# The head of a fused SSM and MLP kernel: x slabs loaded in token halves, a weight block in one load, a bias row first in its queue, a shorter warm-up

## The chip, the cores and the metric

The kernel runs on one core of one Trainium2 chip. The metric is device time in microseconds for one execution, end to end. The profile's own span is about 1.3 us shorter than that time (212.9 against 214.2 for the traced execution of before); spans are compared with spans and times with times. The experiments came in three batches, each on another chip and each with the kernel before measured again, so between batches the ratios are to be compared and not the times.

Names used below: PE is TensorE's matmul stream, PEld its weight loads, DVE is VectorE, ACT is ScalarE, SP and ACT also issue the transfers of the head ("SPq", "ACTq"). A "slab" is 128 of the 640 columns of x; a "W1 block" is the 128 rows of W1 that meet one slab.

## The reference, cut to what matters

For x of 2048 tokens by 640 features, the kernel gives g * a + (1 - g) * b, where b is an MLP and a is a diagonal state-space model:

```python
g = sigmoid((x * gate_w).sum(-1, keepdims=True))
b = gelu(x @ w1 + b1) @ w2 + b2            # w1: 640 x 1728, w2: 1728 x 640
# a: Bu = x @ B_bar.T, h[t] = Lam_bar * h[t-1] + Bu[t], y = 2 Re(h @ C.T) + x * Dskip
```

Everything is bf16 in and out.

## The kernel before: the parts that matter

Work on each engine is put in order at build time by a small scheduler; `op(name, engine, duration, reads, writes, fn, prio)` declares a piece of it, and `load(...)` a transfer. The head of the kernel:

```python
load("xna", "sp", ..., xn[0][:, :, 0:256], x2[0:512, 0:256] ...)       # slabs 0 and 1 of x, 512 tokens
for h in range(2):                                                       # W1 block 0, in two halves of its columns
    load(f"w1_0{h}", "sp", ..., W1sb[:, 0, fs], B_w1[0:128, fs], [("w1", 0, h)], ...)
w1load(1, "sp", 1.3)
w1load(2, "sp", 2)
xtrans(0, range(KN, KD), 3, 1.8)                                         # slabs 2 to 4, transposed by the DMA
w1load(3, "sp", 4)
w1load(4, "sp", 5)
...
def f_warm():                                                            # dummy matmuls, 3328 columns
    for n in (512,) * 6 + (256,):
        t = nc.tensor.matmul(PS[4][:, 0:n], one.broadcast_to([128, 128]), one.broadcast_to([128, n]), ...)
op("warm", "pe", 2.7, (), [("bank", 4)], f_warm, prio=-1000)
# slabs 0 and 1 are transposed on PE: 8 transposes, then copied from PSUM by DVE (3 copies)
for i, (k, c0, c1) in enumerate(((0, 0, 2), (0, 2, 4), (1, 0, 4))):
    ...
# the biases and the SSM's vectors sit in rows of one tile, and one PE transpose makes columns of them:
op("cols", "pe", 0.3, list(ROWS) + ["b1b", "ident"], [("bank", 7)], f_cols, prio=9.5)   # after 9 W1 matmuls
# then 40 matmuls of 512 columns, W1 block by W1 block (k), into 8 PSUM banks (jf):
#   (0,0..6), (1,0..6), (0,7), (1,7), (2,0..7), (3,0..7), (4,0..7)
```

The row tile is filled by five small loads on the ACT queue: three of 5 rows, one of 13 rows (the bias of the first 1664 hidden units), and last a single row for the remaining 64 hidden units, "b1b".

## Time and profile before

| | before |
|---|---|
| time, median of 4 executions | 213.85 us (213.47 to 213.9) |
| profiled span | 212.9 us |
| PE busy | 208.4 us, 98% |
| first W1 matmul | 4.64 us |
| start of the 12th W1 matmul | 8.30 us |

First, the page of the kernel before: busy time of each engine, share of the span, instructions.

```profile
PE 208.4 (98%) x1254; PEld 119.8 (56%) x1264; DVE 188.9 (89%) x262; ACT 111.3 (52%) x201; POOL 2.5 (1%) x10
```

PE is the bound. The chain of waits of the kernel before, in order of time (start, length, what), says where it isn't yet:

```profile
2.60 5.08 DMA rows<-in_B_b_dram
7.68 0.14 issue
7.82 0.22 PE ps L432
8.03 5.18 PE ps L621 x24
13.21 0.05 issue
13.27 1.46 PE ps L621 x6
```

From 2.60 to 7.68 us the chain is one transfer, the bias row b1b, which PE's bias transpose (line 432) waits for. From there to the end it is PE work with gaps of about 0.05 us. So a microsecond saved before about 9 us is worth a microsecond at the end, and nearly nothing else can be gained. The timeline of PE in the head of the kernel before (start, length, then in brackets the idle time before it and what ended it):

```profile
2.01 1.70 PE L401 MATMUL ps<-const-bfloat16-1.0 128*128 128x512 bf16 x4
3.74 0.65 PE L413 MATMUL ps<-ident,xn 128*128 128x128 bf16 x8
4.64 1.04 PE L621 MATMUL ps<-xT,W1sb 128*128 128x512 bf16 x4 [0.25 <-DVE xT L419]
5.85 0.82 PE L621 MATMUL ps<-xT,W1sb 128*128 128x512 bf16 x3 [0.17 <-DMA W1sb<-in_B_w_dram]
6.92 0.61 PE L621 MATMUL ps<-xT,W1sb 128*128 128x512 bf16 x2 [0.25 <-DMA W1sb<-in_B_w_dram]
7.82 0.22 PE L432 MATMUL ps<-ident,rows 128*128 128x128 bf16 x1 [0.29 <-DMA rows<-in_B_b_dram]
7.87 2.32 PE L621 MATMUL ps<-xT,W1sb 128*128 128x512 bf16 x10
```

Line 401 is the warm-up, 413 the transposes of x, 621 the W1 matmuls. Three holes follow the first W1 matmul: for the second half of block 0, for block 1, and for b1b. The brackets are smaller than the holes, because a matmul's recorded end lies some 0.16 us after the next one could have started (379 ns recorded, starts 0.2155 us apart). Counted by starts, the 12th W1 matmul begins 3.66 us after the first (8.30 - 4.64), where eleven matmuls of 0.2155 us and a bias transpose of 0.055 us need 2.43. So 1.24 us are lost in the holes. The view of one line, for the W1 matmuls between 4.5 and 9 us (durations in ns: least, median, largest), gives the speed:

```profile
L621 PE MATMUL ps<-xT,W1sb x15: 377/379/391, 4.6 to 8.9; 128*128 128x512 bf16 x15
```

All 15 take about 379 ns and start 0.2155 us apart when nothing is missing. The transfers, from the DMA view of the kernel before (size, then us from issue to landing; issued at 0.74, 1.25 and 1.79 us):

```profile
xn<-in_A_x_dram SPq DMA_DIRECT2D x1, 256.0 KB, 3.0
W1sb<-in_B_w_dram SPq DMA_DIRECT2D x1, 128.0 KB, 2.8
W1sb<-in_B_w_dram SPq DMA_DIRECT2D x1, 128.0 KB, 4.0
```

### The profile page before, as it was taken

Reading aid. Unit: us, or ns where it says so; the run is one execution under the profiler, and the core shown is the slowest. Engines: PE = TensorE matmul, PEld = TensorE weight load, DVE = VectorE, ACT = ScalarE, POOL = GpSimd, SP = SyncE. Lnnn points to the kernel's source line nnn. Section 1 sums busy time; section 2 is a strip of 40 time slices with the busy share of each in tenths; the row PEclk is TensorE's granted clock in tenths of the full one; section 3 lists DMA queues with packets and bytes.
Section 4 is the critical chain, followed back from the end, with each engine's and each line's share of the span. In section 5 each row is a group of like instructions: output and inputs, shape, how many; then the busy total and the mean of one; then the engine's idle time right before and its main releaser. Section 6 shows DMA issues by size and latency. Waiting matters only on the chain.

```text
span 212.9 us, 3113 instructions
## 1 busy us (share of the span) xinstructions
PE 208.4 (98%) x1254; PEld 119.8 (56%) x1264; DVE 188.9 (89%) x262; ACT 111.3 (52%) x201; POOL 2.5 (1%) x10
## 2 busy tenths in 40 slices
PE   8899999999999999999999999999999999999996
PEld 3344444444467776444466777544446777767773
DVE  2399999999999999999999959999999998999343
ACT  2389556678915324556963233555793444723330
POOL 1000000000000010000000001000000000000000
DMA  5999999998100004100000004000000000000011
GB/s 134 298 284 200 170 208 318 265 222 183 22 0 3 31 31 126 62 0 0 0 3 0 0 34 155 31 31 3 0 0 2 3 31 31 31 3 31 31 34 62
DMA packets 31434, 16.35 MB, mean 77 GB/s; under 512 B 22972, under 2 KB 30652, under 8 KB 31420
## 3 DMA queue, kind: packets, MB, share of 16 engines
q1 hardware_dynamic: 31072, 14.83, 29.2%
q0 software_dynamic: 288, 1.31, 1.9%
q8 instruction: 10, 0.16, 0.3%
q14 instruction: 4, 0.03, 0.0%
q10 hardware_dynamic: 60, 0.01, 0.0%
HBM read 7.63 MB, written 2.62 MB: 48 GB/s over the span
## 4 chain that ended last, share of the span: by engine, by line
PE 95%; DMA 2%; issue 1%; ACTq 1%; POOL 0%; DVE 0%; POOLq 0%
PE ps L771 27%; PE ps L641 22%; PE ps L819 20%; PE ps L684 20%; PE ps L621 3%; DMA rows<-in_B_b_dram 2%; PE ps L785 1%; PE ps L662 1%; ACTq L326 1%; DVE osb L852 0%; POOL io_i L382 0%; PE ps L432 0%; POOL rows L372 0%; POOL st_i L384 0%; POOL st_i L383 0%
## 5 line engine op out<-in xcount | busy, mean ns | idle before, releaser
L771 PE MATMUL ps<-W2sb,Gl 128*128 128x320 bf16 x416 | 59.2, 299 | 0.0
L771 PEld LDWEIGHTS ps<-W2sb,Gl 128*128 128x128 bf16 x416 | 40.3, 98 | 17.1 <-issue 1.1
L641 PE MATMUL ps<-xT,W1sb 128*128 128x512 bf16 x215 | 47.5, 379 | 0.3
L819 PE MATMUL ps<-CT,H 128*128 128x320 bf16 (+2 forms) x320 | 45.4, 299 | 0.0
L724 DVE TENSOR_TENSOR_SCAN W<-atab,V 128x1280 bf16<-128x1280 f32 x16 | 44.3, 2811 | 0.3
L684 PE MATMUL ps<-xT,BT 128*128 128x512 bf16 x196 | 43.1, 379 | 0.3 <-issue 0.2
L819 PEld LDWEIGHTS ps<-CT,H 128*128 128x128 bf16 x320 | 31.3, 98 | 12.2
L799 ACT ACTIVATE E<-ps,g1col 128x320 bf16<-128x320 f32 x32 | 16.3, 526 | 39.7 <-PE ps L771 26.0
L641 PEld LDWEIGHTS ps<-xT,W1sb 128*128 128x128 bf16 x220 | 21.5, 98 | 26.0
L648 ACT ACTIVATE Gl<-ps,cols 128x512 bf16<-128x512 f32 x44 | 29.6, 688 | 10.0 <-PE ps L641 10.0
L684 PEld LDWEIGHTS ps<-xT,BT 128*128 128x128 bf16 x200 | 19.5, 98 | 23.5 <-ACT Gt L670 0.4
L693 ACT ACTIVATE U<-ps 128x512 bf16<-128x512 f32 x40 | 23.8, 597 | 15.0 <-PE ps L684 14.9
L830 ACT ACTIVATE E<-ps,gcol 128x320 bf16<-128x320 f32 x30 | 15.8, 527 | 22.6 <-PE ps L819 22.6
L482 DVE TENSOR_TENSOR osb<-xg,E 128x640 bf16<-128x640 bf16 x15 | 7.3, 487 | 9.2 <-ACT E L830 8.2
L758 ACT ACTIVATE ps<-b2b 128x320 f32<-128x320 bf16 x32 | 14.1, 442 | 1.1
L838 DVE SCALAR_TENSOR_TENSOR xg<-xn,gcol,dsk 128x640 bf16<-128x640 bf16 x16 | 13.9, 883 | 0.4
L598 DVE SCALAR_TENSOR_TENSOR scr<-xn,gwb 128x640 bf16<-128x640 bf16 x16 | 13.2, 823 | 0.4
L482 DVE TENSOR_TENSOR V<-V,W 128x1280 bf16<-128x1280 bf16 x16 | 12.5, 822 | 0.3
L482 DVE TENSOR_TENSOR H<-H,V 128x1280 bf16<-128x1280 bf16 x16 | 12.5, 822 | 0.3
L482 DVE TENSOR_TENSOR V<-mr,U 128x2560 bf16<-128x2560 bf16 x8 | 11.9, 1489 | 0.2
L482 DVE TENSOR_TENSOR H<-c,W 128x2560 bf16<-128x2560 bf16 x8 | 11.9, 1489 | 0.1
L482 DVE TENSOR_TENSOR V<-s,W 128x2560 bf16<-128x2560 bf16 x8 | 11.9, 1485 | 0.0
(79 smaller groups left out, 98.5 us busy)
## 6 DMA issues: line engine op xcount, KB each, us to landing
out_dram<-osb SPq DMA_DIRECT2D x15, 160.0 KB, 1.8
W2sb<-in_B_w_dram SPq DMA_DIRECT2D x1, 2080.0 KB, 9.4
xn<-in_A_x_dram POOLq DMA_DIRECT2D x2, 640.0 KB, 4.7
W1sb<-in_B_w_dram SPq DMA_DIRECT2D x4, 256.0 KB, 4.8
xn<-in_A_x_dram SPq DMA_DIRECT2D x1, 640.0 KB, 8.0
W1sb<-in_B_w_dram SPq DMA_DIRECT2D x1, 480.0 KB, 5.7
W1sb<-in_B_w_dram SPq DMA_DIRECT2D x1, 400.0 KB, 5.8
xn<-in_A_x_dram SPq DMA_DIRECT2D x1, 384.0 KB, 6.2
```

Of the source, the lines that this page charges most:

```text
L482: return inc("dve", nc.vector.tensor_tensor(out=o, in0=a, in1=b, op=o_))
L641: t = nc.tensor.matmul(PS[bank][:, :], W1sb[:, k, jf * 128:(jf + 1) * 128], xT[q][:, k, :], start=(k == 0), stop=(k == KD - 1))
L648: return inc("act", nc.scalar.activation(Gl[q % 2][:, jf, :], PS[bank][:, :], ACT.Gelu_apprx_tanh, bias=b1col[:, jf:jf + 1]))
L684: t = nc.tensor.matmul(PS[bank][:, :], BT[:, ci, kd, k * 128:(k + 1) * 128], xT[q][:, kd, :], start=(kd == 0), stop=(kd == KD - 1))
L693: return inc("act", nc.scalar.activation(dst, src, ACT.Copy, scale=1.0 if ci == 0 else -1.0))
L724: t = inc("dve", nc.vector.tensor_tensor_scan(out=g[:, ci, :], data0=a, data1=v[:, ci, :], initial=0.0, op0=ALU.mult, op1=ALU.add))
L758: return inc("act", nc.scalar.activation(PS[bank][:, 0:HALF], b2b[:, cols], ACT.Copy))
L771: t = nc.tensor.matmul(PS[bank][:, 0:HALF], Gl[q % 2][:, jf, t4 * 128:(t4 + 1) * 128], W2sb[:, jf, cols], start=False, stop=False, skip_gr ...
L799: return inc("act", nc.scalar.activation(E1[c % NE][:, cols], PS[bank][:, 0:HALF], ACT.Copy, scale=g1col[:, c:c + 1]))
L819: t = nc.tensor.matmul(PS[bank][:, 0:n], H[b % NHB][:, ci, k, s * 128:(s + 1) * 128], CT[:, ci, k, cols], start=(i == 0), stop=(i == 2 * K ...
L830: return inc("act", nc.scalar.activation(E2[c % NE][:, cols], PS[bank][:, 0:HALF], ACT.Copy, scale=gcol[:, c:c + 1]))
L838: return inc("dve", nc.vector.scalar_tensor_tensor(out=xg[c % 2][:, :], in0=xn[q % 2][:, c % 4, :], scalar=gcol[:, c:c + 1], in1=dsk[:, :] ...
```

## The change

The intent: let the first transposes start on half of x, have all of W1 block 0 when its matmuls start, and take the bias row out of PE's way. The diff, cut to its core:

```diff
-        load("xna", "sp", "l_xna", xn[0][:, :, 0:KN * 128], x2[0:512, 0:KN * 128]..., ["xna"], 0, dur=0.45, lat=2.0)
         for h in range(2):
-            fs = slice(h * FW // 2, (h + 1) * FW // 2)
-            load(f"w1_0{h}", "sp", f"l_w10{h}", W1sb[:, 0, fs], B_w1[0:128, fs], [("w1", 0, h)], 0.1 + h, ...)
+            load(f"xna{h}", "sp", f"l_xna{h}", xn[0][:, 2 * h:2 * h + 2, 0:KN * 128],
+                 x2[256 * h:256 * h + 256, 0:KN * 128]..., [("xna", h)], 0.1 * h, dur=0.45, lat=2.0)
+        w1load(0, "sp", 1)
@@ the bias row goes to the front of the ACT queue
-             B_b1[nmain:F]..., ["b1b"], prio=-96, dur=0.4)
+             B_b1[nmain:F]..., ["b1b"], prio=-101, dur=0.4)
@@ the warm-up gets shorter: 2944 columns in place of 3328
-            for n in (512,) * 6 + (256,):
-                t = nc.tensor.matmul(PS[4][:, 0:n], ...)
+            for n in (512,) * 5 + (384,):
+                t = nc.tensor.matmul(PS[3][:, 0:n], ...)
-        op("warm", "pe", 2.7, (), [("bank", 4)], f_warm, prio=-1000)
+        op("warm", "pe", 2.4, (), [("bank", 3)], f_warm, prio=-1000)
@@ four groups of two transposes, each with its copy
-        for i, (k, c0, c1) in enumerate(((0, 0, 2), (0, 2, 4), (1, 0, 4))):
+        for i, (k, c0, c1) in enumerate(((0, 0, 2), (1, 0, 2), (0, 2, 4), (1, 2, 4))):
-            op(f"xt{i}", "pe", 0.11 * (c1 - c0), ["xna", "ident"], ...)
+            op(f"xt{i}", "pe", 0.11 * (c1 - c0), [("xna", c0 // 2), "ident"], ...)
@@ the bias transpose after 11 W1 matmuls
-        op("cols", "pe", 0.3, ..., f_cols, prio=9.5)
+        op("cols", "pe", 0.3, ..., f_cols, prio=11.5)
... (the rest adapts the names of what is waited for)
```

More of the change, by code (lines that the diff above doesn't have):

```diff
@@ L353, in bass_gated_mix__ssm_conv_s5__dense_activation_gelu__prompt_kernel @@
         KN = 2
-        load("xna", "sp", "l_xna", xn[0][:, :, 0:KN * 128], x2[0:512, 0:KN * 128].rearrange("(c p) d -> p c d", p=128), ["xna"], 0, dur=0.45, lat=2.0)
         for h in range(2):
-            fs = slice(h * FW // 2, (h + 1) * FW // 2)
-            load(f"w1_0{h}", "sp", f"l_w10{h}", W1sb[:, 0, fs], B_w1[0:128, fs], [("w1", 0, h)], 0.1 + h, dur=0.45, lat=2.0)
+            load(f"xna{h}", "sp", f"l_xna{h}", xn[0][:, 2 * h:2 * h + 2, 0:KN * 128],
+                 x2[256 * h:256 * h + 256, 0:KN * 128].rearrange("(c p) d -> p c d", p=128), [("xna", h)], 0.1 * h, dur=0.45, lat=2.0)
+        w1load(0, "sp", 1)
         w1load(1, "sp", 1.3)
@@ L378, in bass_gated_mix__ssm_conv_s5__dense_activation_gelu__prompt_kernel @@
         load("b1b", "act", "l_b1b", rows[RT:RT + 1, :].rearrange("o (a p) -> o a p", a=2),
-             B_b1[nmain:F].rearrange("(o p) -> o p", o=1).unsqueeze(1).broadcast_to([1, 2, FL]), ["b1b"], prio=-96, dur=0.4)
+             B_b1[nmain:F].rearrange("(o p) -> o p", o=1).unsqueeze(1).broadcast_to([1, 2, FL]), ["b1b"], prio=-101, dur=0.4)
         def f_iota():
@@ L399, in f_warm @@
             t = None
-            for n in (512,) * 6 + (256,):
-                t = nc.tensor.matmul(PS[4][:, 0:n], one.broadcast_to([128, 128]), one.broadcast_to([128, n]), start=True, stop=True)
+            for n in (512,) * 5 + (384,):
+                t = nc.tensor.matmul(PS[3][:, 0:n], one.broadcast_to([128, 128]), one.broadcast_to([128, n]), start=True, stop=True)
             return inc("pe", t)
-        op("warm", "pe", 2.7, (), [("bank", 4)], f_warm, prio=-1000)
-        for i, (k, c0, c1) in enumerate(((0, 0, 2), (0, 2, 4), (1, 0, 4))):
+        op("warm", "pe", 2.4, (), [("bank", 3)], f_warm, prio=-1000)
+        for i, (k, c0, c1) in enumerate(((0, 0, 2), (1, 0, 2), (0, 2, 4), (1, 2, 4))):
             bank = 7 - i
@@ L414, in f_xt @@
                 return inc("pe", t)
-            op(f"xt{i}", "pe", 0.11 * (c1 - c0), ["xna", "ident"], [("bank", bank)], f_xt, prio=-990 + i)
+            op(f"xt{i}", "pe", 0.11 * (c1 - c0), [("xna", c0 // 2), "ident"], [("bank", bank)], f_xt, prio=-990 + i)
             def f_xc(k=k, pt=pt, c0=c0, c1=c1):
@@ L424, in bass_gated_mix__ssm_conv_s5__dense_activation_gelu__prompt_kernel @@
         XK0[0] = [("xT", 0, 0, 0), ("xT", 0, 0, 2)]
-        XK0[1] = [("xT", 0, 1, 0)]
+        XK0[1] = [("xT", 0, 1, 0), ("xT", 0, 1, 2)]
         XT = {q: [("xT", q, k) for k in range(KD)] for q in range(1, NQ)}
@@ L432, in f_cols @@
             return inc("pe", nc.tensor.transpose(psC, rows[:, :], ident[:, :]))
-        op("cols", "pe", 0.3, list(ROWS) + ["b1b", "ident"], [("bank", 7)], f_cols, prio=9.5)
+        op("cols", "pe", 0.3, list(ROWS) + ["b1b", "ident"], [("bank", 7)], f_cols, prio=11.5)
         def f_cols1():
@@ L570, in bass_gated_mix__ssm_conv_s5__dense_activation_gelu__prompt_kernel @@
         load("xnb", "sp", "l_xnb", xn[0][:, :, KN * 128:D], x2[0:512, KN * 128:D].rearrange("(c p) d -> p c d", p=128),
-             [("xn", 0, 0), ("xn", 0, 1)], 32.4, dur=1.0, lat=6.0, reads=["xna"])
+             [("xn", 0, 0), ("xn", 0, 1)], 32.4, dur=1.0, lat=6.0, reads=[("xna", 0), ("xna", 1)])
         load("w2a", "sp", "l_w2a", W2sb[:, 0:NF - 1, :], B_w2[0:nmain, :].rearrange("(j p) d -> p j d", p=128), ["w2a"], prio=33, lat=8.0)
@@ L622, in f_mm @@
                                                       start=(k == 0), stop=(k == KD - 1)))
-                op(f"m1_0_{jf}_{k}", "pe", d_mm(512), XK0[k] + [("w1", k) if k else ("w1", 0, jf // (NW // 2))], [("bank", jf)] ,
+                op(f"m1_0_{jf}_{k}", "pe", d_mm(512), XK0[k] + [("w1", k)], [("bank", jf)] ,
                    f_mm, prio=pe_prio())
@@ L643, in f_mm @@
                     return inc("pe", t)
-                op(f"m1_{q}_{jf}", "pe", KD * d_mm(512), XT[q] + ([("w1", 0, 0), ("w1", 0, 1)] + [("w1", k) for k in range(1, KD)] if jf < NW else [("w1", "r", int(jf * 128 >= FM))]), [("bank", bank)], f_mm, prio=pe_prio())
+                op(f"m1_{q}_{jf}", "pe", KD * d_mm(512), XT[q] + ([("w1", k) for k in range(KD)] if jf < NW else [("w1", "r", int(jf * 128 >= FM))]), [("bank", bank)], f_mm, prio=pe_prio())
                 def f_ge(jf=jf, bank=bank):
```

## The prediction

> **What bounds the kernel.** TensorE. The page gives PE 98% busy of 212.9 us, and the chain of waits is 95% PE: from 7.82 us on it is PE work with issue gaps of 0.05 us, and PE waits for no other engine or transfer. So only the head (to about 9.4 us) can give much, and a microsecond saved there should come off the end.
>
> **The head, from the timeline and the DMA view.** The x load is issued at 0.74 and lands 3.0 us later (3.74); 8 transposes, 3 copies; first W1 matmul 4.64. The halves of W1 block 0 land at 4.05 and 5.8; block 1 at 6.87; block 2 near 7.6; the transposing load of x (slabs 2 to 4) near 9.07. Matmuls follow each other every 0.215 us. PE idles after 4.64: about 0.33 us for the second half of block 0 (until 5.85), 0.42 for block 1 (until 6.92), and 0.46 before the bias transpose, which waits for the single-row bias (issued 2.60, landed 7.68 in the chain). Nine matmuls are done by then; slab 2's first starts at 9.38. Sum: 1.2 us.
>
> **What the change does.**
> 1. x in token halves: the first half should land near 3.2, the second near 3.7. Warm-up loses 384 of 3328 columns (0.32 us at the 0.43 us that 512 take there). xT is ready near 4.4 instead of 4.5. This gains little, because:
> 2. W1 block 0 in one load lands with its last byte: near 5.2 to 5.8, where the second half lands today, since the same bytes stand before it. The first matmul moves *later*, from 4.64 to about 5.5; then 7 run without a break to about 7.0, when block 1 is there (6.87). One gap in place of three.
> 3. The single-row bias goes first in the ACT queue and should land near 3. The bias transpose, now after 11 matmuls (about 7.9), then waits only for the 13-row bias, moved back one place (5.2 before, perhaps 6 to 7.5 now). [...]
> 4. Slab 2 cannot start before its transposing load lands, near 9.05, against 9.38 today. So of 1.2 us at most 0.33 comes through, unless that load lands sooner; its bytes and issue time (3.27) are unchanged.
> 5. Late, the scheduler puts VectorE's last scan behind one combine. That delays the last state by about 1 us (196.8 to 197.8); PE needs it at 205.3, so it costs nothing.
>
> **Risk.** PE now idles from about 4.2 to 5.5, after less warm-up. Matmul spacing was 0.43 us up to 3.3 and 0.215 from 4.64. [...] were the switch missed, the first 7 matmuls would take 0.43 us each, up to 1.5 us lost. I give that 10%.
>
> **Prediction.** 213.6 us (0.25 less), 213.0 to 214.3. Faster by over 2%: 0.01; within: 0.97; slower: 0.02.
>
> **What would show it.** First W1 matmul after 5; no wait for the single-row bias; slab 2's first matmul at 9.05 to 9.3, released by the transposing load; the rest equal. Wrong if block 0 lands by 4.7 or the transposing load before 8.7 (more gain), or if block 0 lands after 6 or PE stays at 0.43 us (loss).

The sum came to 1.2 us of waits, of which at most 0.33 was to come through and 0.25 was predicted.

## The result, and the profile after

| | before | after |
|---|---|---|
| time, median of 4 | 213.85 us (213.47 to 213.9) | 215.38 us (215.03 to 215.78) |
| profiled span | 212.9 us | 213.7 us |
| first W1 matmul | 4.64 us | 5.30 us |
| start of the 12th W1 matmul | 8.30 us | 9.13 us |

The ratio is 1.0076, with a 95% interval from 1.0052 to 1.01. Ratios are the mean time of one kernel's fast runs over that of the other's in the same rounds, so they are not quite the ratio of the medians. The two traced executions lie closer together than the medians: the one of before took 214.2 us, more than its median, and the one of the change was the fastest of its four (215.03). So the traces show 0.8 us of a loss of about 1.5. Its chain of waits:

```profile
0.74 0.45 SPq L326
1.19 0.06 issue
1.25 3.22 DMA xn<-in_A_x_dram
4.47 0.05 issue
4.52 0.41 PE ps L413 x2
4.93 0.02 issue
4.95 0.30 DVE xT L419
5.25 0.05 issue
5.30 3.94 PE ps L621 x11
9.24 0.06 PE ps L432
9.30 4.96 PE ps L621 x23
```

The bias row has left the chain; its place is taken by the second half of x, landing at 4.47. After that everything is PE. But look at the piece at 5.30: eleven matmuls in 3.94 us, where eleven should take about 2.5 with the last one's tail (10 times 0.2155 and 0.379). The timeline of PE after:

```profile
3.19 0.63 PE L413 MATMUL ps<-ident,xn 128*128 128x128 bf16 x4
4.52 0.61 PE L413 MATMUL ps<-ident,xn 128*128 128x128 bf16 x4 [0.70 <-DMA xn<-in_A_x_dram]
5.30 3.94 PE L621 MATMUL ps<-xT,W1sb 128*128 128x512 bf16 x11 [0.17 <-DVE xT L419]
9.08 0.22 PE L432 MATMUL ps<-ident,rows 128*128 128x128 bf16 x1
```

No hole is left between 5.30 and 9.08, and PE reads as fully busy. The view of one line says why that is no good (after, W1 matmuls between 4.5 and 9 us), and the timeline of the weight loads below it shows the rhythm:

```profile
L621 PE MATMUL ps<-xT,W1sb x11: 379/607/635, 5.3 to 8.9; 128*128 128x512 bf16 x11
```

```profile
6.13 0.15 PEld L621 LDWEIGHTS ps<-xT,W1sb 128*128 128x128 bf16 x1 [0.28 <-issue]
6.55 0.15 PEld L621 LDWEIGHTS ps<-xT,W1sb 128*128 128x128 bf16 x1 [0.28 <-issue]
6.98 0.15 PEld L621 LDWEIGHTS ps<-xT,W1sb 128*128 128x128 bf16 x1 [0.28 <-issue]
7.41 0.15 PEld L621 LDWEIGHTS ps<-xT,W1sb 128*128 128x128 bf16 x1 [0.28 <-issue]
8.21 0.53 PEld L621 LDWEIGHTS ps<-xT,W1sb 128*128 128x128 bf16 x3 [0.23 <-issue]
```

The loads come every 0.427 us, and then, from 8.21 on, three within 0.53 us. Seven W1 matmuls ran at half speed (about 0.427 us apart in place of 0.2155), the speed of the warm-up, whose matmuls of 512 columns also take about 631 ns and come every 0.427 us in both kernels. In the kernel before, PE reached full speed among the transposes, at about 3.85 us (the last six of the eight start 0.055 to 0.067 us apart, the first four of the change 0.106 to 0.107); in this execution at about 8.15 us.

The account (rounded) of the 0.83 us by which the 12th W1 matmul is later (9.13 against 8.30):

| | us |
|---|---|
| first W1 matmul later (5.30 - 4.64) | +0.66 |
| seven matmuls at half speed: from 5.30 to 8.21 is 2.91 us, at 0.2155 each it would be 1.51 | +1.40 |
| the holes of before, gone | -1.24 |
| sum | +0.82 |

The rest of the two traces runs in parallel: the spans differ by 0.8. The change did remove the holes that it aimed at. It lost more by a slow clock and a later start. In this trace the slow clock alone (1.40 us) takes back more than the holes gave (1.24 us).

The profile's windows view has a column for the granted clock of TensorE. After, for the stretch with the slow matmuls, it reads (us, length, busy times of PE, PEld, DVE, ACT and POOL with counts, clock, DMA share, GB/s):

```profile
5.30:8.20 2.90, 2.90 (x7) 1.03 (x8) 0.15 (x1) 0.00 (x0) 0.00 (x0) 1.00 1.17 242
```

The clock column says 1.00 and PE is busy all the time. Half speed is to be seen here only in the time of one matmul (607 to 635 ns for the first six), or in the distance between two (0.427 us).

### The profile page after: what moved, and what is told of

The parts are those of the page before. It is cut to its first block, busy times and chain, and to the rows that moved or that the text cites. A ratio compares the mean times of both kernels' runs of the same rounds, so it can differ in the third digit from the quotient of the medians.

```text
span 213.7 us, 3113 instructions
## 1 busy us (share of the span) xinstructions
PE 209.3 (98%) x1253; PEld 120.6 (56%) x1263; DVE 189.3 (89%) x263; ACT 111.3 (52%) x201; POOL 2.5 (1%) x10
## 4 chain that ended last, share of the span: by engine, by line
PE 96%; DMA 2%; issue 0%; DVE 0%; SPq 0%
PE ps L771 27%; PE ps L641 22%; PE ps L819 20%; PE ps L684 20%; PE ps L621 5%; DMA xn<-in_A_x_dram 2%; PE ps L785 1%; PE ps L662 1%; DVE osb L852 0%; SPq L326 0%; PE ps L413 0%; DVE xT L419 0%; PE ps L432 0%
## 5 line engine op out<-in xcount | busy, mean ns | idle before, releaser
L482 DVE TENSOR_TENSOR W<-mi,U 128x2560 bf16<-128x2560 bf16 x8 | 11.9, 1485 | 0.0
```

The source lines that it names most:

```text
L482: return inc("dve", nc.vector.tensor_tensor(out=o, in0=a, in1=b, op=o_))
```

## The experiments

Theory A: TensorE starts at half speed and goes to full speed at a moment that depends on how busy it was before. The change's shorter warm-up, with idle time around the two groups of transposes, misses the moment that the kernel before catches. What the traces show of it are the two speeds (matmuls of 512 columns 0.427 us apart, then 0.2155) and the moment between them, called "the switch" here. "The clock" is the name for that speed; its cause is not shown. Theory A also had a length of stretch and a share of it that has to be busy. No run shows those.

Rival 1: the loss comes from the transfers, above all from the second half of x (4.47). Rival 2 (theory B in one text): the clock, but by the length of the first unbroken warm-up alone, or by the split of the transposes alone. All kernels gave correct results. For each, the order of instructions on every engine was compared with its parent's, and only what the diff says had moved, with one exception: in `e6_bias_first_only` the scheduler also moved three combines on VectorE and one copy on ACT, as it did in the change itself.

### The change with the warm-up of before

```diff
-            for n in (512,) * 5 + (384,):
+            for n in (512,) * 6 + (256,):
```

> The changed kernel with the warm-up of before: 3328 columns in place of 2944, nothing else. Theory (the clock of TensorE is still at half rate when the first W1 matmuls run, because the warm-up stops too early): the W1 matmuls follow each other every 0.215 us from the first (near 5.3), the 11 before the bias transpose take 2.4 us and not 3.8, and the kernel takes about 213.4 us, 1.4 to 2 us less than the change and some 0.4 less than before. Rival 1 (the late second half of x is what costs): the same 215.2 us as the change. Rival 2 (not the length but the idle time of about 1 us between the transposes of the two halves keeps the clock down): also 215.2 us, with matmuls every 0.43 us.

Measured: 213.42 us (213.25 to 213.69, 4 runs) against 213.88 of before in the same rounds, ratio 0.9979 (0.9961 to 0.9997). The line of the W1 matmuls and PE's timeline of this run:

```profile
L621 PE MATMUL ps<-xT,W1sb x19: 376/379/379, 4.9 to 8.9; 128*128 128x512 bf16 x19
```

```profile
4.93 2.53 PE L621 MATMUL ps<-xT,W1sb 128*128 128x512 bf16 x11 [0.37 <-DVE xT L419]
7.30 0.22 PE L432 MATMUL ps<-ident,rows 128*128 128x128 bf16 x1
```

Eleven matmuls now take 2.53 us in place of 3.94, and the 12th starts at 7.36 in place of 9.13. 384 dummy columns, worth 0.32 us of PE time, took 2 us off the changed kernel. This is what theory A expects and not what rival 1 does: the loads, and the PSUM bank of the warm-up, are those of the change. The second half of x landed at 3.96 here and at 4.47 in the change's first trace, so part of the gain (0.37 us in the start of the first W1 matmul) may be chance in the transfers; the other 1.4 us is the speed.

### Before with the short warm-up

```diff
-            for n in (512,) * 6 + (256,):
+            for n in (512,) * 5 + (384,):
```

> The kernel before with the short warm-up of the change (2944 columns), nothing else. Theory: the clock misses its switch here too; the first 7 or so W1 matmuls come every 0.43 us and fill the waits for transfers that stood there, so the loss is part of 1.5 us: about 214.5 us (214.2 to 215.2). Rival 1 (late x half) and rival 2 (idle time between two groups of transposes): x still comes in one load, so 213.85 us, matmuls every 0.215 us.

Measured: 213.97 us (213.6 to 214.15), ratio 0.9999 (0.9977 to 1.0022). By its time this would speak against theory A. The trace speaks otherwise:

```profile
L621 PE MATMUL ps<-xT,W1sb x15: 379/379/634, 4.8 to 8.8; 128*128 128x512 bf16 x15
```

```profile
4.75 3.07 PE L621 MATMUL ps<-xT,W1sb 128*128 128x512 bf16 x9
7.66 0.22 PE L432 MATMUL ps<-ident,rows 128*128 128x128 bf16 x1
```

The first five W1 matmuls did run 0.36 to 0.43 us apart, and the switch came at about 6.7 us. The slow matmuls simply filled the holes: 9 of them last from 4.75 to the bias transpose at 7.66, which came no later than before (7.82), where PE had been done early and stood waiting for b1b until 7.68 (here PE's timeline shows no idle time before that transpose). So my expectation of 214.5 was wrong in the size: the kernel before paid nothing for a switch at 6.7 us, because it is waiting for data in the same microseconds. (A switch as late as those of the change, after 8 us, was not seen on it.) The change removed those waits, and so exposed the clock.

### A longer warm-up still

```diff
-            for n in (512,) * 5 + (384,):
+            for n in (512,) * 8:
```

> The changed kernel with 8 warm-up matmuls of 512 columns (4096), so that PE is busy without a break until about 4.0 us and the first transposes come after it. Theory: full rate from before the first W1 matmul, about 213.4 us; if e1 was still slow, this one is fast, which would say that the warm-up has to be longer than the one of before when nothing follows it. Rival 1: 215.2 us or more, as the first half of x is transposed later still.

Measured: 213.80 us (213.67 to 214.08), ratio 0.9997 (0.9979 to 1.0015). The W1 matmuls are at full speed from the first, but the first starts at 5.53 us, released by the copies of transposes that began only at 4.15; W1 block 0 had landed at 5.39. So the clock is repaired here too; the 0.4 us more than the expected 213.4 is a start that is 0.6 us later than in `e1_long_warm`. A warm-up can also be too long, as this one is.

### The change with x in one load

```diff
-            load(f"xna{h}", ...)            # two halves
+        load("xna", "sp", "l_xna", xn[0][:, :, 0:KN * 128], x2[0:512, 0:KN * 128]..., [("xna", 0), ("xna", 1)], 0, ...)
```

> The changed kernel with x in one load again (W1 block 0 in one load, bias first, short warm-up stay). Theory: the warm-up ends near 3.2 and nothing runs until x lands at 3.7, so the clock stays down: 7 or so W1 matmuls every 0.43 us, about 215 us. Rival 1 (the split of x costs, by its late second half): the first W1 matmul follows block 0 at about 5.1, at full rate, and the kernel takes 213.4 to 213.7 us. Rival 2 (idle time between the groups of transposes): full rate as well, as the transposes are together again.

Measured: 215.64, 216.41, 216.38 and 213.39 us, ratio 1.0073 (1.001 to 1.0136). In its trace the first W1 matmul starts at 5.11, but

```profile
5.11 4.74 PE L621 MATMUL ps<-xT,W1sb 128*128 128x512 bf16 x11 [0.43 <-DVE xT L419]
```

eleven matmuls take 4.74 us: all of them at half speed. So neither the late half of x (rival 1) nor the split of the transposes (rival 2) is what costs. And one execution of the same program, on the same chip, took 213.39 us. That its switch came early is likely, but it was not the traced one; three traces of one program follow below.

### The change with its gaps filled

```diff
             op(f"xt{i}", "pe", 0.11 * (c1 - c0), [("xna", c0 // 2), "ident"], [("bank", bank)], f_xt, prio=-990 + i)
+            # after the 2nd and the 4th group of transposes: dummy matmuls of 512 + 256, and of 512 columns
```

Cut from the next text are theory A's stretch and share, and the latest moment of the switch, which rested on them. The 213.6 us is left as the author's estimate: it can no longer be derived from the text. What the run still tests is whether filling the gaps brings an early switch.

> The changed kernel with its short warm-up, and three more dummy matmuls: 512 and 256 columns after the transposes of the first half of x, 512 after those of the second, so that PE is never idle for long between 0.78 us and the first W1 matmul. Theory A [...]: the gaps were what kept the share down[...]; about 213.6 us (213.3 to 214.2), no run above 214.5. Theory B (only the length of the first unbroken warm-up counts): the clock stays down as in the change, 215.2 us or more.

Measured: 213.74 us (213.58 to 214.27, 6 runs), ratio 0.9994 (0.9979 to 1.001). No run was slow. The warm-up is the short one of the change; what differs is that PE was busy from 0.78 to 5.2 us with at most 0.26 us idle at a time:

```profile
3.61 0.84 PE L421 MATMUL ps<-const-bfloat16-1.0 128*128 128x512 bf16 x2
4.51 0.46 PE L413 MATMUL ps<-ident,xn 128*128 128x128 bf16 x4
5.24 2.55 PE L630 MATMUL ps<-xT,W1sb 128*128 128x512 bf16 x11
```

Here the second half of x landed at 4.46, as late as in the change's first trace, and the first W1 matmul started at 5.24, nearly as late (5.30). The time of eleven matmuls is 2.55 in place of 3.94 us. This is the cleanest pair: same loads, same landing, same start, and the difference is the clock. It also speaks against theory B, because the leading warm-up is no longer than the change's. One could object that warm-up, transposes and dummy matmuls together now run without a break from 0.78 to 4.25 us. Other traces answer that, with transposes counted as work: the change ran without a break for 2.83 us (0.78 to 3.61) and stayed at half speed, the kernel before ran so for only 2.73 us, stood for 0.24, and was at full speed by 3.85; and `e2_before_short_warm` switched in the middle of its W1 matmuls with no unbroken run longer than 2.41 us. So in these traces the length of one unbroken run is not what counts.

### Each part of the change alone, on the kernel before

The bias row first, and the bias transpose after 11 matmuls:

```diff
-             ..., ["b1b"], prio=-96, dur=0.4)
+             ..., ["b1b"], prio=-101, dur=0.4)
-        op("cols", ..., f_cols, prio=9.5)
+        op("cols", ..., f_cols, prio=11.5)
```

> The kernel before with the bias part of the change alone: single-row bias load first in the ACT queue, bias transpose after 11 matmuls. If the wait of 0.46 us for that load was worth something by itself: the bias transpose near 7.9 with 11 matmuls done (9 before), slab 2 at 9.0 to 9.1 (9.38 before), about 213.5 us (0.3 to 0.4 less). If the wait only hid another: 213.85 us.

Measured: 213.46 us (213.23 to 214.02, 6 runs) against 213.94, ratio 0.998 (0.9964 to 0.9996). The bias transpose came at 7.50 with 11 matmuls done, where before it came at 7.82 with 9. (PE still stood for about 0.26 us before it.) That is the useful part of the change, and it gives about as much as all of it with a working clock (`e1_long_warm`).

W1 block 0 in one load:

```diff
-            load(f"w1_0{h}", ...)           # two halves
+        w1load(0, "sp", 1)
```

> The kernel before with W1 block 0 in one load alone. First W1 matmul from 4.64 to about 5.1, the waits between the first nine gone, but the bias transpose still waits for its row until about 7.7: no change, 213.85 us within 0.2. If the single load brings the later transfers forward (slab 2's x and W1 blocks 1 to 4), still none, since the bias row stands in front.

Measured: 213.89 us, ratio 0.9996 (0.9982 to 1.001): no change, as expected. PE's timeline shows the wait that swallows it:

```profile
4.81 2.19 PE L621 MATMUL ps<-xT,W1sb 128*128 128x512 bf16 x9
7.35 0.22 PE L432 MATMUL ps<-ident,rows 128*128 128x128 bf16 x1 [0.35 <-DMA rows<-in_B_b_dram]
```

One detail was not as I had thought. The single load of block 0 (256 KB) landed at 4.41 us, where the second of two halves with the same bytes before it had landed at 5.8. In the trace of before, packets move slowly between about 3.4 and 4.5 us (42 to 84 GB/s, against some 350 in the microsecond before); the single load got through sooner, and block 1 came at 6.35 (6.87 in the trace of before). Why there is such a slow time was not studied.

The whole change without the halves of x, with the long warm-up:

```diff
-            load(f"xna{h}", ...)            # two halves
+        load("xna", ...)                    # one load
-            for n in (512,) * 5 + (384,):
+            for n in (512,) * 6 + (256,):
```

> The changed kernel with x in one load and the warm-up of before (so e1 without the halves of x). If the halves are worth time when the clock is up: slower than e1's 213.4 us by 0.3 or more. If not: 213.4 us, the first W1 matmul at about 5.1, when block 0 lands. PE still idles from about 4.5 to 5.1 here, so by theory A some runs may be 1 to 2 us longer with matmuls at 0.43 us.

Measured: 213.92 us (213.52 to 215.07, 6 runs), ratio 1.0008 (0.9986 to 1.0029). The traced execution ran at full speed, with the first W1 matmul at 4.83, and yet its bias transpose came at 7.86, after an idle 0.23 us that the timeline puts down to the load of a bias row (`0.23 <-DMA rows<-in_B_b_dram`). Two of the six runs were at 214.55 and 215.07; they have no trace, and a late switch is only a likely reason for them. Against `e1_long_warm` (0.9979) the intervals overlap, and the rounds are not the same; whether the halves of x are worth anything stays open.

### The long warm-up and no gap at all

```diff
-            for n in (512,) * 5 + (384,):
+            for n in (512,) * 6 + (256,):
+            # and one dummy matmul of 512 columns after the 4th group of transposes
```

> The changed kernel with the warm-up of before (3328 columns) and one dummy matmul of 512 columns after the transposes of the second half of x: no gap from 0.78 us to the first W1 matmul. Theory A [...]: [...] about 213.4 us (213.2 to 213.9), as e1, with no run above 214. If the filler delays the first W1 matmul, it is 0.1 to 0.2 us slower than e1.

Measured: 213.74 us (213.24 to 214.03, 6 runs), ratio 0.9996 (0.9979 to 1.0013). The traced run (213.24) was at full speed from about 3.4 us and had its first W1 matmul at 4.91. It did not beat `e1_long_warm`; one run was 0.03 above the limit that I had set. As the version to keep I would take `e1_long_warm`, or `e6_bias_first_only`, which is the simpler; each is 0.2% faster than before, with an interval that just leaves out 1.

### No warm-up

```diff
-            for n in (512,) * 5 + (384,):
+            for n in (128,):
```

> The changed kernel with the warm-up cut to one matmul of 128 columns. Theory A: [...] 216.5 us (215.5 to 219). If it equals the change (215.2 us), the short warm-up of the change buys nothing at all in most runs. A theory that the clock is not the cause expects no change from 215.2.

Measured: 215.57 us (214.85 to 216.44), ratio 1.0086 (1.0059 to 1.0114). Eleven matmuls at half speed, the switch at about 9.8 us:

```profile
5.38 4.73 PE L621 MATMUL ps<-xT,W1sb 128*128 128x512 bf16 x11 [0.17 <-DVE xT L419]
```

The changed kernel measured in the same rounds took 215.27 us. Eleven slow matmuls are fewer than I had expected. In most of its executions the change's warm-up of 2944 columns bought nothing that these runs can tell: the change's own traces below have nine slow matmuls.

### The change once more, and a third time

> The changed kernel unaltered, for a second trace. Theory A [...]: the switch falls at another time than the 8.1 us of the first trace [...], and the kernel's time follows it: each W1 matmul before it adds 0.21 us. Median about 215.3, and single runs between 213.4 and 216.4. If the moment is fixed by the program, the switch is at 8.1 again.

> The changed kernel unaltered, a third trace, as e11: another moment of the switch, and a time that follows it.

Measured: 215.37, 215.17, 213.63 and 215.71 us for the first (ratio 1.005, 1.0013 to 1.0088), 215.16 us for the second, a single run. Their lines of the W1 matmuls, first and second:

```profile
5.19 4.39 PE L621 MATMUL ps<-xT,W1sb 128*128 128x512 bf16 x11 [0.17 <-DVE xT L419]
```

```profile
5.04 4.30 PE L621 MATMUL ps<-xT,W1sb 128*128 128x512 bf16 x11 [0.17 <-DVE xT L419]
```

The switch was at about 8.95 and 8.65 us, after 8.15 in the first trace, so one program switches at different moments. Counted by starts, nine W1 matmuls were slow in each of these two, which is 1.86 and 1.76 us lost, where the first trace had seven and 1.40 us. Of nine executions of the unaltered change, eight took 215.03 us or more and one took 213.63. That the fast one had an early switch is likely, but it was not the traced one.

### How long PE stood idle before the switch: an estimate

A trace that shows the switch at time T shows also how long PE stood idle between 0.78 us, where the warm-up starts, and T. The idle times below are estimates from the starts of the matmuls, with 0.427 us for 512 columns and 0.107 us for a transpose at half speed:

| trace | switch at | idle before it |
|---|---|---|
| e9_long_warm_fill | 3.4 | 0 us |
| before | 3.85 | 0.2 us |
| e2_before_short_warm | 6.7 | 0.7 us |
| after | 8.15 | 1.3 us |
| e12_change_third | 8.65 | 1.0 us |
| e11_change_again | 8.95 | 1.2 us |
| e4_whole_x | 9.6 | 1.1 us |
| e10_no_warm | 9.85 | 3.7 us |

In the other six traces every W1 matmul from the first was at full speed (376 to 390 ns), so the switch came before 4.67 to 5.53 us, where the first one starts.

The two traces with 0.2 us or less switched early, the one with 0.7 us in the middle, the five with 1.0 us or more late. Among the three traces of the change and `e4_whole_x` the order doesn't follow the idle time, so the idle time alone doesn't give the moment. No run varied it by itself, and neither a length of work nor a busy share that is enough is shown by these runs.

For the change's design the same starts say this: its 2944 columns kept PE busy for 2.41 us, until 3.19, and the first transposes until 3.61; then PE stood for 0.91 us, and for 0.38 more before the first W1 matmul. The 3328 columns of before took 2.73 us, and 0.24 us later the transposes came.

## Why the prediction was wrong

The prediction was 213.6 us, 213.0 to 214.3; measured were 215.38. Point by point:

- **What bounds the kernel, and that only the head matters: right.** The spans differ by 0.8 us, and the 12th W1 matmul is already 0.83 later.
- **Step 1, halves of x near 3.2 and 3.7: half right.** The first landed at 3.04, the second at 4.47 (3.96 to 4.55 in other traces with halves), later than the whole load of before (3.70 in its landing records).
- **Step 2, W1 block 0 between 5.2 and 5.8, first W1 matmul about 5.5: close in this trace, but for another reason.** Block 0 landed at 5.12 (and at 4.41 alone on the kernel before); the first matmul, at 5.30, waited for the copy of the late half of x.
- **Step 3, the bias row near 3, the 13-row bias between 6 and 7.5, no wait: right** (3.01 and 7.34). The same single row, with the same shape, landed at 7.68 when last and at 3.01 when first, and the 13-row bias went from 5.21 to 7.34 when it became the last. So the place in the queue is what these traces show to matter.
- **Step 4, the transposing load near 9.05 holds slab 2 back: not tested by the change.** It landed at 8.66, and PE got to slab 2 only at 10.21. With the clock repaired (`e1_long_warm`) it landed at 8.23 and PE got there at 8.44, without a break, so it was not the limit there either. The gain of `e1_long_warm` (1.0 us between the two spans, 0.46 between the medians of the same rounds) is larger than my 0.33, because that load did land sooner, as I had left open.
- **Step 5, VectorE's scan behind one combine costs nothing: right.** The last state was ready at about 198.6 (197.8 predicted), PE needed it at 205.99.
- **The risk: this is the step that failed.** "Were the switch missed, the first 7 matmuls would take 0.43 us each, up to 1.5 us lost. I give that 10%." The loss came in that form (matmuls 0.427 us apart). The chance was wrong: all three traced executions of the change show it, and eight of its nine executions took 215.03 us or more. The size was right in the first trace (7 matmuls, 1.40 us), but by luck: in the other two it was nine matmuls and 1.86 and 1.76 us, because the moment of the switch, and not the count of block 0's matmuls, ends the slow ones. I took the length of the warm-up and transposes in all as what counts, and let the transposes make up for the 384 columns. What I didn't do was count the idle time: 0.91 us between the two groups of transposes and 0.38 before the first W1 matmul, where the kernel before stood for 0.24 us before its switch. Nor did I see that the three holes of before were a cushion for a late switch, which `e2_before_short_warm` shows.

## What to carry to other kernels

A warm-up is part of the schedule: when it is trimmed to make room for an earlier start, work out how long TensorE stands idle around it, as in the estimate above, and fill the waits for data with dummy matmuls. In the traces here they delayed nothing: the first W1 matmul came at 5.24 and 4.91 us with them (`e5_fill_gaps`, `e9_long_warm_fill`) and at 5.30 and 4.93 without (the change, `e1_long_warm`). Waits for data at the start of a kernel can hide a slow clock, as they did in `e2_before_short_warm` (ratio 0.9999 with a switch at 6.7 us), so a change that removes them can expose it; look at the time of one matmul, and not at the busy share, before believing that PE is at its limit. And a kernel whose times fall into two groups, 213.4 and 215 to 216 us here, should be traced more than once.
